# First weights in longer runs, fp32 filler matmuls, split and moved casts, and a reordered last product in a fused attention and FFN kernel

## The chip, the core and the metric

The kernel runs on one core of one Trainium2 chip. The time is that of the device in microseconds (us) for one execution of the whole kernel. A core has five engines that the text names: PE (TensorE, with its weight loads PEld), DVE (VectorE), ACT (ScalarE), POOL (GpSimd) and SP (SyncE), which here issues every DMA. PSUM is the memory that PE writes to; a "bank" below is one 2 KB slice of it in each of 128 partitions.

## The reference

Attention within chunks of 64 tokens, then a bilinear feed-forward layer on what it gives:

```python
# q, k, v: (8, 8, 576, 64) = batch, heads, sequence, head dim
scores = (1/8) * q_c @ k_c.T                     # per chunk of 64 tokens: 64 x 64
attn   = exp(scores - max) / (sum + 1e-9)
x      = (attn @ v_c) -> (4608 tokens, 512)      # heads side by side
out    = ((x @ w_a) * (x @ w_b)) @ w_out         # w_a, w_b: 512 x 1536, w_out: 1536 x 512
```

Inputs and outputs are fp32. The kernel multiplies in bf16 and accumulates in fp32.

## The kernel before, in words

**Tiling.** The 4608 tokens are nine blocks of 512. A block is two units of 256 tokens, and a unit is two groups of 128 tokens (two chunks of 64). Blocks 0 to 3 and 5 to 8 each take 512 tokens of one batch entry; block 4 collects the last 64 tokens of all eight, so that the loads of units 8 and 9 go in pieces of 64 partitions (`runs`), twice as many DMAs as elsewhere.

**Attention of a unit.** Q and k are loaded as fp32, cast to bf16 and turned, so that the head dimension lies on partitions. From unit 4 on a DMA transpose (`transpose_dma`, L215) turns them; units 2 and 3 are loaded two tokens to a partition (`load_pairs`) and turned on PE (`transpose_pairs`, L193, with copies out of PSUM in `evacuate_pairs`); block 0, units 0 and 1, is loaded four tokens to a partition and goes through its own `quad_` and `half_` functions. Scores go to PSUM tile PS (L233; L339 in block 0), ACT takes the exponential, PE sums it over keys with a matrix of ones (L250; `half_sums`, L351, in block 0), ACT takes the logarithm of the sums and the exponential of its negative, and DVE multiplies the values' product (PA; L266, L373) by this inverse (`normalise`, L285; `half_normalise`, L383). The result is xT, the transposed input of the next layer.

**Feed-forward.** `ffn` multiplies xT by one 128-wide tile of w_b and of w_a (four matmuls of 512 columns each, L397), ACT copies b out of PSUM (L408), and DVE multiplies a by it (L409). There are twelve such tiles in a block. Blocks 0 and 1 then multiply by w_out plainly (L419). From block 2 on `outs_fast` forms the output in seven half-size products in place of eight (L478), from sums of w_out that POOL made earlier (`sum_wo`) and sums of the products that DVE makes (`sum_ab`). In it ACT copies the products m3 and m4 to SBUF, POOL adds them to w (L496), DVE adds p1 to w, and further sums on DVE and POOL give the four quarters of the output. All products take their banks in turn from the ring F of four, so a bank must have been read before the fourth product after it.

**Order.** The program is written out by hand; every engine executes its instructions in the order written, and waits on semaphores. `slot(uv, us)` puts sums and values of unit uv and scores of unit us between two feature tiles. `cast_unit` casts q, k and v of a unit on POOL, `turn_unit` and `load_unit` issue DMAs on SP. In blocks 2 to 8 a slot at position i is followed by the casts of the next unit at i+1 and by its turn and the load of a further unit at i+3 (L836 to L843). SP issues in one order, so a DMA that waits holds up all later ones.

**Start.** SP issues q and k of block 0 (eight DMAs), v (eight), and the weights of pairs 0 and 1 (a pair is two feature tiles) in eight DMAs of 256 KB with runs of 128 columns, 512 bytes; pair 2 follows in two of 512 KB with runs of 256 columns, 1 KB. Weights go into a ring of ten staging slots, `wst`, and POOL casts them tile by tile (`land_half`, L171). PE meanwhile runs filler matmuls on zeros (`fill`, L522): eight at the start, one after the first transposes, four before the second values, two before the first feed-forward product. In units 2 and 3 casts are spread over POOL and DVE: DVE casts k of unit 2 in one piece (L732).

## Time and profile before

| | us |
|---|---|
| five runs | 316.63, 319.50, 319.71, 320.34, 320.47; median 319.71 |
| the profiled execution | 320.47 (one of the five) |
| its span, first to last instruction | 318.6 |
| outside the span | 1.87 |
| PE busy | 304.2 (95%) |
| DVE / ACT / POOL busy | 183.8 / 133.0 / 125.2 |
| DMA, mean over the span | 173 GB/s |
| mean granted clock of PE | 0.992 |

A group or timeline line reads: start, duration, engine, line of the program, operation, output and input, count, and in brackets how long the engine stood idle before it and what released it. A wait line gives the engine and line that waited, what it waited for, the total in us, how often, and the longest. A stretch line gives, for a window of time, busy us and count of each engine in the order PE, PEld, DVE, ACT, POOL, then the granted clock, the busy share of the DMA engines and GB/s. Busy times of matmuls that overlap in the pipeline are merged.

In the second view of the page, 40 slices of the span, the DMA engines show 90% or more in every slice from 8 to 151 us, and less after that. PE shows 70 to 79% in the first two slices and in the fifteenth (111.5 to 119.5 us), 40% in the last, and 90% or more in all others.

### The profile page before, as it was taken

How to read it: one execution, taken by the hardware profiler on the slowest of the kernel's cores; microseconds unless marked ns; L12 is line 12 of the kernel's file. 1: busy time of each engine (PE TensorE's matmuls, PEld its weight loads, DVE VectorE, ACT ScalarE, POOL GpSimd, SP SyncE). 2: the span in 40 equal slices, each digit the busy share in tenths (PEclk: the TensorE clock that was granted, in tenths of full speed). 3: DMA queues.
4: the chain of work that ended last, by engine and by line, in shares of the span. 5: the costliest groups of instructions: out<-in, count | busy, mean ns of one | idle time of the engine just before them, and what ended most of it. 6: DMA issues, size and time to landing. Idle time of an engine off the chain costs nothing.

```text
span 318.6 us, 7278 instructions
## 1 busy us (share of the span) xinstructions
PE 304.2 (95%) x2881; PEld 176.4 (55%) x2915; DVE 183.8 (58%) x368; ACT 133.0 (42%) x224; POOL 125.2 (39%) x161
## 2 busy tenths in 40 slices
PE   7799999999999979999999999999999999999994
PEld 3434446864444466446744674467446744674474
DVE  3433434534457743866587658764876476656662
ACT  3722217645236521645164516451645164413320
POOL 3657868977472145500660056005600400040022
PEclk9999999999999998999999999999999999999999
DMA  7999999999999999999299639962600210020003
GB/s 234 266 316 379 404 281 249 232 278 229 225 190 235 211 205 249 254 241 221 99 228 189 151 75 177 257 157 91 174 2 2 88 47 0 2 98 37 0 0 135
DMA packets 146899, 55.01 MB, mean 173 GB/s; under 512 B 126256, under 2 KB 140848, under 8 KB 146864
## 3 DMA queue, kind: packets, MB, share of 16 engines
q1 hardware_dynamic: 146864, 54.54, 68.9%
q8 instruction: 23, 0.38, 0.5%
q14 instruction: 12, 0.10, 0.1%
HBM read 37.75 MB, written 9.44 MB: 148 GB/s over the span
## 4 chain that ended last, share of the span: by engine, by line
PE 66%; SPq 17%; DMA 12%; issue 2%; POOL 2%; DVE 0%; POOLq 0%; DVEq 0%
PE F L397 43%; PE F L478 19%; SPq L123 10%; DMA wst<-in_moe_w_a_dram 5%; DMA f<-in_v_dram 3%; DMA f<-in_q_dram 3%; SPq L153 2%; SPq L131 2%; DMA qkT<-qkb 2%; SPq L146 2%; PE F L250 1%; SPq L139 1%; PE PS L233 1%; PE PA L266 1%; PE F L419 1%
## 5 line engine op out<-in xcount | busy, mean ns | idle before, releaser
L397 PE MATMUL F<-xT,wa 128*128 128x512 bf16 (+1 forms) x458 | 112.2, 366 | 0.8 <-POOL wa L171 0.3
L397 PE MATMUL F<-xT,wb 128*128 128x512 bf16 (+1 forms) x433 | 110.2, 366 | 1.7 <-POOL wb L171 0.6
L408 ACT CAST bsb<-F 128x512 bf16<-128x512 f32 (+1 forms) x115 | 64.0, 557 | 107.6 <-PE F L397 107.4
L409 DVE TENSOR_TENSOR ab<-F,bsb 128x512 bf16<-128x512 f32 (+1 forms) x115 | 75.4, 656 | 55.0 <-PE F L397 48.3
L397 PEld LDWEIGHTS <-wa 128*128 128x128 bf16 x460 | 44.7, 98 | 49.6 <-POOL wa L171 2.1
L397 PEld LDWEIGHTS <-wb 128*128 128x128 bf16 x460 | 43.3, 98 | 45.5 <-POOL wb L171 1.9
L496 POOL TENSOR_TENSOR part<-part 128x256 f32<-128x256 f32 x14 | 10.1, 724 | 130.3 <-ACT part L504 130.3
L171 POOL CAST qkb<-f 128x1024 bf16<-128x1024 f32 (+1 forms) x37 | 35.9, 980 | 26.5 <-DMA f<-in_k_dram 16.5
L478 PEld LDWEIGHTS <-wst 128*128 128x128 bf16 x420 | 41.5, 99 | 7.4 <-issue 2.2
L478 PE MATMUL F<-wst 128*128 128x256 bf16 x252 | 34.5, 276 | 2.0 <-DVE part L496 2.0
L285 DVE TENSOR_TENSOR xT<-PA,inv 128x512 bf16<-128x512 f32 x32 | 21.8, 684 | 16.6 <-ACT inv L280 16.6
L496 DVE TENSOR_TENSOR osb<-F,part 128x256 f32<-128x256 f32 x56 | 22.3, 420 | 10.7 <-POOL part L496 10.2
L171 POOL CAST vb<-f 128x1024 bf16<-128x1024 f32 (+2 forms) x22 | 19.9, 910 | 13.4 <-DMA f<-in_v_dram 9.5
L496 POOL TENSOR_TENSOR part<-part,osb 128x256 f32<-128x256 f32 x28 | 19.7, 725 | 12.2 <-DVE osb L496 12.2
L478 PE MATMUL F<-wst,ab 128*128 128x256 bf16 x168 | 24.0, 281 | 0.0
L276 ACT ACTIVATE lns<-F 128x512 f32<-128x512 f32 x32 | 17.4, 595 | 10.9 <-PE F L250 10.9
L419 PE MATMUL F<-wo,ab 128*128 128x512 bf16 x92 | 21.3, 379 | 0.4 <-issue 0.3
L496 DVE TENSOR_TENSOR part<-F,part 128x256 f32<-128x256 f32 x14 | 5.9, 425 | 26.4 <-POOL part L496 26.4
L467 DVE TENSOR_TENSOR wst<-ab 128x512 bf16<-128x512 bf16 x42 | 20.9, 497 | 0.0
L244 ACT ACTIVATE E<-PS 128x1024 bf16<-128x1024 f32 (+1 forms) x20 | 18.8, 942 | 4.9 <-PE PS L233 2.8
L478 PE MATMUL F<-wo,wst 128*128 128x256 bf16 x168 | 20.7, 273 | 0.0
L466 DVE TENSOR_TENSOR wst<-ab 128x512 bf16<-128x512 bf16 x42 | 20.1, 477 | 0.0
(48 smaller groups left out, 194.3 us busy)
## 6 DMA issues: line engine op xcount, KB each, us to landing
out_dram<-osb SPq DMA_DIRECT2D x31, 256.0 KB, 2.0
f<-in_q_dram SPq DMA_DIRECT2D x28, 256.0 KB, 4.0
f<-in_k_dram SPq DMA_DIRECT2D x28, 256.0 KB, 4.2
f<-in_v_dram SPq DMA_DIRECT2D x28, 256.0 KB, 4.4
wst<-in_moe_w_out_dram SPq DMA_DIRECT2D x6, 512.0 KB, 8.5
f<-in_v_dram SPq DMA_DIRECT2D x16, 128.0 KB, 3.6
wst<-in_moe_w_b_dram SPq DMA_DIRECT2D x4, 512.0 KB, 6.7
wst<-in_moe_w_a_dram SPq DMA_DIRECT2D x4, 512.0 KB, 7.9
```

The costliest lines, as they stand in the source:

```text
L123: eng.dma_start(out=t[p:p + n, g * 512:(g + 1) * 512].rearrange("p (h d) -> p h d", h=H), in_=src[b, :, s0:s0 + n, :].transpose([1, 0, 2]),)
L171: eng.tensor_copy(out=out, in_=in_)
L244: nc.scalar.activation(out=e[:, :, s], in_=PS[:, :, s], func=AF.Exp, scale=scale)
L285: nc.vector.tensor_tensor(out=x.rearrange("p m (g c t) -> p c g m t", g=2, c=2)[:, cl], in0=PA[:, cl, :].rearrange(shape, g=2, m=4), in1=i ...
L397: nc.tensor.matmul(bank[:, 0:n], w[ft // 2][ft % 2][:, kt, :], x[:, kt, us[0] * 256:us[0] * 256 + n], start=(kt == 0), stop=(kt == NKT - 1),)
L408: nc.scalar.copy(out=bT[:, 0:n], in_=banks[0][:, 0:n])
L409: nc.vector.tensor_tensor(out=ab[ft][:, us[0] * 256:us[0] * 256 + n], in0=banks[1][:, 0:n], in1=bT[:, 0:n], op=MULT)
L419: nc.tensor.matmul(o, ab[ft][:, tg * 128:(tg + 1) * 128], wo[ft // 2][:, ft % 2, :], start=(ft == 0), stop=(ft == NFT - 1),)
L466: nc.vector.tensor_tensor(out=y[:, 0:2], in0=a[:, 0:2], in1=a[:, 2:4], op=ADD)
L467: nc.vector.tensor_tensor(out=y[:, 2:4], in0=a[:, 1:3], in1=a[:, 0:4:3], op=SUB)
L478: nc.tensor.matmul(o, a(i)[:, c:c + 128], b(i), start=(i == 0), stop=(i == NP - 1))
L496: eng.tensor_tensor(out=out, in0=in0, in1=in1, op=op)
```

## The change

- The weights of pairs 0 and 1 are loaded in runs of 256 columns, as pair 2's were. Those of pair 0 are split by partitions in two DMAs each, b in 120 + 8, a in 104 + 24. The ring of staging slots starts at slot 4.
- `zero` is fp32 instead of bf16, so the fillers are fp32 matmuls. Eight become four, the one after the first transposes gets 128 columns, one is added before the first values, four become two, two become one.
- `half_sums` sums a whole half unit in four matmuls of 512 columns instead of eight of 256.
- The cast of k of unit 2 is split in two halves, on DVE and on ACT.
- The cast of v of unit 9, one instruction of POOL, is issued four steps later: after both fast output products of block 2, ahead of the casts of unit 10.
- In the last `outs_fast` (block 8, t = 1) the products come in another order: m3, m4, the two that need only these, then p1 and the last two. p1 is added on DVE to y1 and y2 instead of to w. Every other `outs_fast` keeps its order.

```diff
@@ -64,7 +64,7 @@
 
     identity = buf("identity", [128, 128], BF16)
     ones = buf("ones", [128, 64], BF16)
-    zero = buf("zero", [128, 512], BF16)
+    zero = buf("zero", [128, 512], FP32)
 
     NF32 = 3
     f32 = [[buf(f"f32_{i}_{x}", [128, 1024], FP32) for x in range(3)] for i in range(NF32)]
@@ -97,7 +98,7 @@
     asum = asum.rearrange("p (i n t) -> p i n t", i=NP, n=5)
     part = buf("part", [128, 2, 5, HF], FP32)
 
-    state = {"f": 0, "b": 0, "o": 0, "w": 0}
+    state = {"f": 0, "b": 0, "o": 0, "w": 4}
 
     def ring(name, bufs):
         i = state[name]
@@ -148,12 +149,14 @@
                 in_=v[0, 4 * hu:4 * hu + 4, g * 128:(g + 1) * 128, :].transpose([1, 0, 2]),
             )
 
-    def load_w(src, c0, n, eng):
+    def load_w(src, c0, n, eng, cut=128):
         st = ring("w", wst)
-        eng.dma_start(
-            out=st[:, 0:NKT * n].rearrange("p (kt c) -> p kt c", kt=NKT),
-            in_=src[:, c0:c0 + n].rearrange("(kt r) c -> r kt c", r=128),
-        )
+        for r in (slice(0, cut), slice(cut, 128)):
+            if r.start < 128:
+                eng.dma_start(
+                    out=st[r, 0:NKT * n].rearrange("p (kt c) -> p kt c", kt=NKT),
+                    in_=src[:, c0:c0 + n].rearrange("(kt r) c -> r kt c", r=128)[r],
+                )
         return st
 
     def load_wo(i, eng):
@@ -174,12 +177,15 @@
     def cast_qk(u, x, eng):
         copy(eng, qkb[u % 2][:, x, :], f32[u % NF32][x])
 
-    def cast_pairs(u, x, eng):
-        copy(
-            eng,
-            qkb[u % 2][:, x, :].rearrange("p (r h d) -> p h r d", r=2, h=H),
-            f32[u % NF32][x].rearrange("p (h r d) -> p h r d", h=H, r=2),
-        )
+    def cast_pairs(u, x, *engs):
+        n = 2 // len(engs)
+        for i, eng in enumerate(engs):
+            r = slice(n * i, n * i + n)
+            copy(
+                eng,
+                qkb[u % 2][:, x, :].rearrange("p (r h d) -> p h r d", r=2, h=H)[:, :, r],
+                f32[u % NF32][x].rearrange("p (h r d) -> p h r d", h=H, r=2)[:, :, r],
+            )
 
     def cast_v(u, eng, pieces=1):
         n = 1024 // pieces
@@ -344,14 +350,13 @@
                         stop=True,
                     )
 
-    def half_sums(hu, mm, SU):
-        s = slice(mm * 256, mm * 256 + 256)
+    def half_sums(hu, SU):
         for j in range(2):
             for cl in range(2):
                 nc.tensor.matmul(
-                    SU[j * 64:j * 64 + 64, cl, s],
+                    SU[j * 64:j * 64 + 64, cl, :],
                     ones[cl * 64:cl * 64 + 64, :],
-                    E[hu][cl * 64:cl * 64 + 64, j, s],
+                    E[hu][cl * 64:cl * 64 + 64, j, :],
                     start=True,
                     stop=True,
                 )
@@ -495,6 +500,24 @@
         def add(eng, out, in0, in1, op=ADD):
             eng.tensor_tensor(out=out, in0=in0, in1=in1, op=op)
 
+        if K == NBLK - 1 and t == 1:
+
+            A.copy(out=m3, in_=product(of_ab(0, 0), of_wsum(2)))
+            A.copy(out=m4, in_=product(of_ab(1, 1), of_wsum(3)))
+            add(G, w, m3, m4)
+            add(V, oa[:, HF:DM], product(of_asum(0), of_wo(1, 1)), m3)
+            add(G, y1, w, oa[:, HF:DM], SUB)
+            add(V, ob[:, 0:HF], product(of_asum(1), of_wo(0, 0)), m4)
+            add(G, y2, w, ob[:, 0:HF], SUB)
+            p1 = product(of_asum(4), of_wsum(4))
+            store(K, 2 + t, ob, 0, HF)
+            add(V, y1, p1, y1)
+            add(V, y2, p1, y2)
+            add(V, oa[:, 0:HF], product(of_asum(3), of_wsum(1)), y1)
+            store(K, t, oa)
+            add(V, ob[:, HF:DM], product(of_asum(2), of_wsum(0)), y2)
+            store(K, 2 + t, ob, HF)
+            return
         A.copy(out=m3, in_=product(of_ab(0, 0), of_wsum(2)))
 
         p4 = product(of_ab(1, 1), of_wsum(3), None, range(NP - 1))
@@ -508,19 +531,21 @@
         add(G, y1, w, oa[:, HF:DM], SUB)
         add(V, ob[:, 0:HF], product(of_asum(1), of_wo(0, 0)), m4)
         add(G, y2, w, ob[:, 0:HF], SUB)
-        halves = K == NBLK - 1 and t == 1
-        if halves:
-            store(K, 2 + t, ob, 0, HF)
         add(V, oa[:, 0:HF], product(of_asum(3), of_wsum(1)), y1)
         store(K, t, oa)
         add(V, ob[:, HF:DM], product(of_asum(2), of_wsum(0)), y2)
-        store(K, 2 + t, ob, HF if halves else 0)
-
-    def fill(n, bank=None):
-
-        for _ in range(n):
+        store(K, 2 + t, ob)
+
+    def fill(times, bank=None, n=512):
+
+
+        for _ in range(times):
             nc.tensor.matmul(
-                PA[:, 0, :] if bank is None else bank, zero[:, 0:128], zero, start=True, stop=True
+                PA[:, 0, 0:n] if bank is None else bank[:, 0:n],
+                zero[:, 0:128],
+                zero[:, 0:n],
+                start=True,
+                stop=True,
             )
 
     staged = {}
@@ -544,23 +569,18 @@
         for hu in range(2):
             load_half_v(hu, nc.sync)
 
-        def queue_half(i, h, ns):
-            for n in ns:
-                src = moe_w_a if n == "a" else moe_w_b
-                staged[n, i, h] = load_w(src, i * 256 + h * 128, 128, nc.sync), 0, 128
-
-        def queue_w(i):
-            for n, src in (("b", moe_w_b), ("a", moe_w_a)):
-                st = load_w(src, i * 256, 256, nc.sync)
+        def queue_w(i, cuts=(128, 128)):
+            for n, src, cut in (("b", moe_w_b, cuts[0]), ("a", moe_w_a, cuts[1])):
+                st = load_w(src, i * 256, 256, nc.sync, cut)
                 for h in range(2):
-                    staged[n, i, h] = st, h * 128, 256
+                    staged[n, i, h] = st, h * 128
 
         def land_half(n, i, h, eng):
-            st, c, w = staged[n, i, h]
+            st, c = staged[n, i, h]
             copy(
                 eng,
                 (wa if n == "a" else wb)[i][h],
-                st[:, 0:NKT * w].rearrange("p (kt c) -> p kt c", kt=NKT)[:, :, c:c + 128],
+                st.rearrange("p (kt c) -> p kt c", kt=NKT)[:, :, c:c + 128],
             )
 
         def land_w(i):
@@ -574,18 +594,18 @@
         def land_wo(i):
             copy(G, wo[i], staged["o", i].rearrange("p (f c) -> p f c", f=2))
 
-        for i in range(2):
-            for h in range(2):
-                queue_half(i, h, "ba")
+
+        queue_w(0, (120, 104))
+        queue_w(1)
         queue_w(2)
 
 
-        fill(8)
+        fill(4)
         quad_cast(0, 0, V)
         quad_turn(0, 0, A)
         quad_cast(0, 1, V)
         quad_turn(0, 1, V)
-        fill(1)
+        fill(1, n=128)
         for m in range(1, 4):
             for x in range(2):
                 quad_cast(m, x, G)
@@ -606,27 +626,26 @@
         quad_scores(2)
         expo(1, 0)
         quad_turn(3, 1, V)
-        half_sums(0, 0, PA)
-        half_sums(0, 1, PA)
+        half_sums(0, PA)
         half_log(PA)
         quad_scores(3)
         expo(1, 1)
         inverse(0)
+        spare = F[2]
+        fill(1, spare)
         half_values(0)
         for mm in range(2):
             half_normalise(0, mm)
-        half_sums(1, 0, PS)
-        half_sums(1, 1, PS)
+        half_sums(1, PS)
         half_log(PS)
         half_inverse(1, 0)
         half_inverse(1, 1)
         B0 = nextF(), nextF()
-        spare = F[2]
-        fill(4, spare)
+        fill(2, spare)
         half_values(1)
         for mm in range(2):
             half_normalise(1, mm)
-        fill(2, spare)
+        fill(1, spare)
         for of in "ba":
             ffn_products(0, 0, (0, 1), (0, 1), B0, of)
         for kt in range(2, NKT):
@@ -729,7 +748,7 @@
         cast_pairs(3, 1, G)
         some_sums(2)
         cast_unit(3, (2,))
-        cast_pairs(2, 1, V)
+        cast_pairs(2, 1, V, A)
         load_unit(5, (0,))
         o = nextF(), nextF()
         for ft in range(NFT):
@@ -837,7 +856,10 @@
                 if i in slots and slots[i] - 1 < NU:
                     slot(slots[i] - 1, slots[i] if slots[i] < NU else None)
                 if i - 1 in slots:
-                    cast_unit(slots[i - 1] + 1)
+
+                    cast_unit(slots[i - 1] + 1, (0, 1) if slots[i - 1] == 8 else (0, 1, 2))
+                if i - 5 in slots:
+                    cast_unit(slots[i - 5] + 1)
                 if i - 3 in slots:
                     turn_unit(slots[i - 3] + 1)
                     load_unit(slots[i - 3] + 3)
```

## The prediction, made before the changed kernel ran

> **What bounds the kernel now.** I read the page's busy shares first, then PE's waits, then the timeline round each wait, then the clock by stretch.
>
> ```profile
> PE 304.2 (95%) x2881; PEld 176.4 (55%) x2915; DVE 183.8 (58%) x368; ACT 133.0 (42%) x224; POOL 125.2 (39%) x161
> ```
>
> PE is the bound: time can only come from PE's idle time, from PE work that runs slowly, or from what lies after PE's last instruction. Of the waits from 40 to 120 us, three are for another engine or a DMA:
>
> ```profile
> PE F L478 <- DVE part L496: 2.0, 1, 2.0
> PE F L193 <- DVE osb L429: 0.7, 1, 0.7
> PE PS L233 <- DMA qkT<-qkb: 0.5, 2, 0.3
> ```
>
> The long one lies in the first fast output product of block 2. The timeline of POOL and PE there:
>
> ```profile
> 111.49 1.04 POOL L171 CAST qkb<-f 128x1024 bf16<-128x1024 f32 x1 [6.59 <-DMA f<-in_k_dram]
> 116.01 1.04 POOL L171 CAST vb<-f 128x1024 bf16<-128x1024 f32 x1 [3.48 <-DMA f<-in_v_dram]
> 117.01 0.72 POOL L496 TENSOR_TENSOR part<-part 128x256 f32<-128x256 f32 x1
> ...
> 118.24 0.81 PE L478 MATMUL F<-wst 128*128 128x256 bf16 x6 [2.00 <-DVE part L496]
> 118.89 2.25 PE L478 MATMUL F<-wst,ab 128*128 128x256 bf16 x11
> ```
>
> POOL's sum w = m3+m4 stands in POOL's order behind the cast of unit 9's v, and that cast waits 3.48 us for its DMA. Until w is there VectorE keeps a PSUM bank, and PE stands. The last line is the second half of the price: 11 matmuls in 2.25 us (205 ns each), where the same 11 take 1.36 us elsewhere. The clock by stretch says why:
>
> ```profile
> 118.00:120.00 2.00, 1.76 (x13) 1.44 (x13) 1.27 (x4) 0.00 (x0) 1.40 (x2) 0.80 1.11 252
> 120.00:122.00 2.00, 2.00 (x11) 1.34 (x10) 0.42 (x1) 0.37 (x1) 0.01 (x1) 0.50 1.07 331
> 122.00:124.00 2.00, 2.00 (x17) 1.67 (x16) 0.34 (x1) 0.37 (x1) 0.72 (x1) 0.85 1.07 172
> ```
>
> The column before the last two is the granted clock: it is halved for about 3.4 us after the stall. This pair of output products runs from 112.14 to 125.14, 13.0 us, where the chain that ended last shows 9.17 us for each later pair. So the place costs 3.83 us: 2.0 waited, 1.8 slow.
>
> The front is a second matter:
>
> ```profile
> 1.19 3.60 PE L522 MATMUL PA<-zero 128*128 128x512 bf16 x8 [1.19 <-DVE zero L536]
> 4.57 1.06 PE L316 MATMUL F<-identity,qkb 128*128 128x128 bf16 x8
> 5.43 0.64 PE L522 MATMUL PA<-zero 128*128 128x512 bf16 x1
> 6.42 0.46 PE L339 MATMUL PS<-qkT 64*64 64x64 bf16 x16 [0.36 <-DVE qkT L171]
> ```
>
> Eight fillers start 427 ns apart and hold PE until 4.57; q of the first quad has been cast by 3.88. From there the attention of unit pair 0 is a chain of short steps (6.42 to 16.86, VectorE's second normalisation), and weights arrive beside it: block 0's first six feature tiles wait several times for a cast that waits for a DMA, the last ending at 25.45. From there PE is dense until 44.9.
>
> **The change part by part.**
>
> *v of unit 9 cast later.* POOL's order becomes q, k of unit 9, the six sums of both output products, then v. The k cast ends at 112.53; w needs both ACT copies, at 114.57. So w runs at 114.6 to 115.3, VectorE's sum at 115.4 to 115.8, and the bank is wanted at 112.14 + 6 x 0.655 = 116.07. The wait goes, and with it the slow stretch: -3.83. Next to be late is the k cast (2.1 us of slack) and then the transposing DMA of unit 9. Behind the moved cast stand on POOL q and k of unit 10, wanted some 15 us later; v of unit 9 itself is first read at the second slot of block 3, about 13 us after. The transposing DMA stands on SP behind the first output's two stores, and those behind unit 10's v loads (issued until 118.60), which PE doesn't hold: it can issue at about 119.7 instead of 120.95 and, with the median 5.6 us to landing, lands at 125.3 (124.2 with the shortest, 4.5). PE now wants it at 129.38-3.83 = 125.55. Cost 0 taken, 0 to 1.5 us possible.
>
> *Fillers.* `zero` becomes fp32, twice the bytes: its memset goes from 0.27 to about 0.54 us, PE starts at 1.46. No fp32 matmul is in the trace. The nearest row is the bf16 filler, 427 ns cold: if an fp32 filler took that, four end at 3.2 and the front gains up to 1.3 us. [...] The 256-column sums joined to 512 stream the same columns (8 in 0.41): 0, between -0.1 and +0.1. [...]
>
> *First weights.* Pairs 0 and 1 (2.1 MB) come in 1 KB runs instead of 512 B. Before, the stretch 14 to 22 us moved 234 to 315 GB/s, the 1 KB stretch 22 to 26 us 351 to 360: 2.1 MB at 280 takes 7.5, at 350 6.0. The records of landing also show each transfer's sixteenth part 0.6 to 1.4 us behind the fifteenth. [...] The last weights of pair 2, at 24.72, land at about 12.4 + 3.15 MB / 340 GB/s + 0.6 = 22.3; the first `a` at about 16.2, cast by 16.8. [...] Front: +0.8, from -1.2 to +2.2. What is gained on DMA pulls later loads forward, and the ring starting at slot 4 takes SP's waits for casts away (2.4 and 0.9 us); PE doesn't see either.
>
> *k of unit 2.* VectorE's cast took 1.35 us (44.15) and stood ahead of two bank copies (1.27), for which the second transpose waited 0.67. Half of it takes about 0.43 to 0.68 (its 128x512 cast takes 0.43); ACT, idle for 8.47 us there, does the other in about 0.58. -0.6; with the front late the wait would have gone by itself, so it is -0.6 either way, once.
>
> *Lag absorbed.* PE then is 0.2 late at 63.85 and 108.3, where it waited 0.29 and 0.18 for transposing DMAs: -0.2, so PE reaches 112.1 unchanged.
>
> *Last output product.* Before, VectorE's chain POOL w, VectorE w, POOL y1, y2, VectorE ends at 315.81, with the last matmul done at about 314.5. Now p1 comes fifth, POOL's sums run during it, and after the last product only one VectorE add is left: three adds (0.4 each) from about 314.0 end at 315.2, and the stores, 0.33 each plus gaps on SP, follow. -0.45, from -0.7 to +0.1.
>
> Sum: -3.83 + 0.8 - 0.6 - 0.2 - 0.45 = **-4.3 us**. The profiled execution took 320.47 us (span 318.6) and is the slowest of the five; the difference carried to their median, 319.71, gives **315.4**. Changes under 1% (3.2 us) can hardly be told from none here: the five runs reach from 316.63 to 320.47.
>
> **The rivals.**
> *The fillers are shorter* (two passes, or the clock rises at once), and weights gate the front: -1.2 for +0.8, transposing DMAs absorb little since DMA is earlier too: about 313.5. For it: the front was DMA-bound. [...] 0.15.
> *A new wait takes the stall's place*: the transposing DMA of unit 9 lands 1 us after PE wants it, and a second half-clock stretch follows: +2, 317.5. For it: parity within 0.3 us by my count. 0.17.
> *The stall stays*, because k of unit 9 (ready 2.1 us early) slips behind PE: 319. 0.04.
> *Slower*: the filler itself. [...] 0.07.
>
> **How the numbers follow.** My case has 0.57, 314.0 to 316.8 by its own bounds. The range, 313.3 to 318.0, takes in the first two rivals. Under 316.5: most of my case and the first rival, 0.64; above 322.9: the slower rival, 0.07; between: 0.29.
>
> **What would show it.** Right: no PE wait for `part` in block 2, the POOL cast of `vb` after both products' sums, clock 1.00 from the front to the end, every pair of fast products 9.17; fp32 fillers about 1.7 us apart cold and 0.85 at full clock, transposes from about 7; weights of pair 2 landed by 22.5 and no PE wait for `wa`; no wait of L193 for `osb`. Wrong: transposes at or before 4.6 (first rival), a wait for `qkT` near 125.5 (second), the half clock beyond 9 us (slower).

## The result and the profile after

The changed kernel takes 317.82 us (median of 38 runs, 316.16 to 320.33), the kernel before 319.08 (75 runs, 316.02 to 322.73). The comparison gives a ratio of 0.9983, 95% interval 0.9967 to 1.0: about 0.5 us gained, no difference that counts. The medians lie further apart, 1.26 us, because the ratio compares means and leaves out runs more than 1.5% above the fastest of their kernel, nine of the kernel before and none of the changed one; the means of all runs are 319.09 and 318.22, 0.9 us apart. The prediction was 315.4, which is 4.3 us under the first median of before, 319.71.

In the two profiled executions the gain is larger: 320.47 us before, 317.68 after, spans 318.6 and 315.9. That gap between the profiles and the medians is half of this case. First the busy shares of the kernel after, from its page:

```profile
PE 305.2 (97%) x2877; PEld 177.6 (56%) x2910; DVE 184.3 (58%) x369; ACT 133.7 (42%) x225; POOL 124.8 (40%) x161
```

PE's waits, in the kernel after, whole span (who waits, for what, total us, times, longest):

```profile
PE PS L345 <- DVE qkT L174: 1.5, 3, 0.6
PE PA L543 <- DVE zero L561: 1.4, 1, 1.4
PE F L402 <- POOL wa L174: 1.3, 1, 1.3
PE PS L345 <- ACT qkT L172: 0.7, 1, 0.7
PE F L424 <- issue: 0.3, 2, 0.2
```

The waits for `part`, for `osb` and for the transposing DMAs (`qkT` by DMA) are no longer in the list; from the first plain output product on, only the two short waits for issue are left in it. What has grown is the third line, the first cast of `wa`: 1.3 us, where the list of before had 0.3 for all casts of `wa`. Lines of the program have moved by five or so: L402 is the feature tile, L483 the fast output product, L424 the plain one, L501 its sums, L174 the casts on POOL.

POOL and PE at the fast products of block 2, timeline of the kernel after:

```profile
111.04 1.04 POOL L174 CAST qkb<-f 128x1024 bf16<-128x1024 f32 x1 [7.31 <-DMA f<-in_k_dram]
116.09 0.72 POOL L501 TENSOR_TENSOR part<-part 128x256 f32<-128x256 f32 x1 [4.01 <-ACT part L527]
117.69 1.41 POOL L501 TENSOR_TENSOR part<-part,osb 128x256 f32<-128x256 f32 x2 [0.87 <-DVE osb L501]
120.68 0.73 POOL L501 TENSOR_TENSOR part<-part 128x256 f32<-128x256 f32 x1 [1.58 <-ACT part L527]
122.27 1.41 POOL L501 TENSOR_TENSOR part<-part,osb 128x256 f32<-128x256 f32 x2 [0.87 <-DVE osb L501]
123.63 1.04 POOL L174 CAST vb<-f 128x1024 bf16<-128x1024 f32 x1
```

POOL's sum w now waits only for ACT's copy, and the cast of unit 9's v comes after all sums. The clock there, in windows of 2 us (the granted clock is the third column from the end):

```profile
118.00:120.00 2.00, 2.00 (x21) 1.79 (x19) 0.85 (x2) 0.37 (x1) 1.10 (x2) 1.00 1.02 235
120.00:122.00 2.00, 2.00 (x21) 1.78 (x20) 0.56 (x2) 0.37 (x1) 0.73 (x1) 1.00 1.01 313
122.00:124.00 2.00, 1.95 (x14) 1.27 (x13) 1.23 (x4) 0.18 (x1) 1.73 (x3) 1.00 1.08 238
```

The pair runs from 113.59 to 122.76, 9.17 us for 13.0. The front of PE, from the timeline of the kernel after:

```profile
1.45 6.47 PE L543 MATMUL PA<-zero 128*128 128x512 f32 x8 [1.45 <-DVE zero L561]
7.75 0.61 PE L322 MATMUL F<-identity,qkb 128*128 128x128 bf16 x8
...
16.06 1.98 PE L543 MATMUL F<-zero 128*128 128x512 f32 x4
...
19.53 0.38 PE L402 MATMUL F<-xT,wb 128*128 128x512 bf16 x1
21.19 0.60 PE L402 MATMUL F<-xT,wa 128*128 128x512 bf16 x2 [1.27 <-POOL wa L174]
...
22.49 1.03 PE L402 MATMUL F<-xT,wb 128*128 128x512 bf16 x4
```

and POOL beside it:

```profile
16.93 0.61 POOL L174 CAST wb<-wst 128x512 bf16<-128x512 f32 x1 [2.06 <-DMA wst<-in_moe_w_b_dram]
20.52 0.61 POOL L174 CAST wa<-wst 128x512 bf16<-128x512 f32 x1 [2.98 <-DMA wst<-in_moe_w_a_dram]
```

An fp32 filler leaves two records, so eight records are four fillers. They hold PE until 7.75. The attention then ends at 19.85 (VectorE's second normalisation, 16.86 before), but the first `a` is cast only from 20.52, where it was 15.82. PE stands for it, and the second feature tile starts at 22.49 for 18.30.

The difference of the two profiled executions by stretch, from the starts of the same work in both:

| stretch | before | after | difference | predicted |
|---|---|---|---|---|
| start to first plain output product | 38.41 | 41.48 | +3.07 | +0.8 |
| to block 1 (k of unit 2) | 15.35 | 14.53 | -0.82 | -0.6 |
| to the fast products of block 2 | 58.38 | 57.58 | -0.80 | -0.2 |
| these two products | 13.00 | 9.17 | -3.83 | -3.83 |
| block 3 to the end | 193.46 | 193.14 | -0.32 | -0.45 |
| span | 318.6 | 315.9 | -2.7 | -4.3 |

### The profile page after: what moved, and what is told of

It reads as the page before. It is cut to its first block, busy times and chain, and to the rows that moved or that the text cites. A ratio compares the mean times of both kernels' runs of the same rounds, so it can differ in the third digit from the quotient of the medians.

```text
span 315.9 us, 7269 instructions
## 1 busy us (share of the span) xinstructions
PE 305.2 (97%) x2877; PEld 177.6 (56%) x2910; DVE 184.3 (58%) x369; ACT 133.7 (42%) x225; POOL 124.8 (40%) x161
## 4 chain that ended last, share of the span: by engine, by line
PE 89%; SPq 4%; DMA 2%; issue 1%; ACT 1%; POOL 1%; POOLq 0%; DVEq 0%; DVE 0%
PE F L402 59%; PE F L483 19%; PE F L424 6%; DMA wst<-in_moe_w_a_dram 2%; SPq L147 2%; PE F L256 2%; PE PS L239 2%; PE PA L272 1%; SPq L140 1%; POOL part L501 0%; SPq L156 0%; ACT lns L282 0%; ACT inv L286 0%; ACT qkT L172 0%; PE F L199 0%
## 5 line engine op out<-in xcount | busy, mean ns | idle before, releaser
L402 PE MATMUL F<-xT,wa 128*128 128x512 bf16 (+1 forms) x460 | 112.4, 366 | 1.6 <-POOL wa L174 1.3
L402 PE MATMUL F<-xT,wb 128*128 128x512 bf16 (+1 forms) x431 | 109.9, 366 | 1.2
L402 PEld LDWEIGHTS <-wa 128*128 128x128 bf16 x460 | 44.9, 98 | 50.0 <-POOL wa L174 1.8
L402 PEld LDWEIGHTS <-wb 128*128 128x128 bf16 x460 | 43.5, 98 | 44.7 <-issue 0.6
L501 POOL TENSOR_TENSOR part<-part 128x256 f32<-128x256 f32 x14 | 10.1, 724 | 131.0 <-ACT part L527 130.0
L174 POOL CAST qkb<-f 128x1024 bf16<-128x1024 f32 (+1 forms) x37 | 36.0, 983 | 28.7 <-DMA f<-in_k_dram 15.7
L483 PEld LDWEIGHTS <-wst 128*128 128x128 bf16 x420 | 41.1, 98 | 4.8
L483 PE MATMUL F<-wst 128*128 128x256 bf16 x252 | 33.3, 273 | 0.0
L501 DVE TENSOR_TENSOR osb<-F,part 128x256 f32<-128x256 f32 x56 | 22.3, 420 | 10.9 <-POOL part L501 9.4
L501 POOL TENSOR_TENSOR part<-part,osb 128x256 f32<-128x256 f32 x28 | 19.7, 725 | 11.4 <-DVE osb L501 11.3
L174 POOL CAST vb<-f 128x1024 bf16<-128x1024 f32 (+2 forms) x22 | 19.9, 910 | 7.4 <-DMA f<-in_v_dram 7.4
L483 PE MATMUL F<-wst,ab 128*128 128x256 bf16 x168 | 22.8, 273 | 0.0
L424 PE MATMUL F<-wo,ab 128*128 128x512 bf16 x92 | 21.3, 379 | 0.4 <-issue 0.3
L250 ACT ACTIVATE E<-PS 128x1024 bf16<-128x1024 f32 (+1 forms) x20 | 18.8, 942 | 4.8 <-PE PS L239 2.5
L483 PE MATMUL F<-wo,wst 128*128 128x256 bf16 x168 | 20.6, 273 | 0.0
L501 DVE TENSOR_TENSOR part<-F,part 128x256 f32<-128x256 f32 x15 | 6.4, 425 | 21.4 <-POOL part L501 21.4
```

What stands on the lines that cost most here:

```text
L174: eng.tensor_copy(out=out, in_=in_)
L250: nc.scalar.activation(out=e[:, :, s], in_=PS[:, :, s], func=AF.Exp, scale=scale)
L402: nc.tensor.matmul(bank[:, 0:n], w[ft // 2][ft % 2][:, kt, :], x[:, kt, us[0] * 256:us[0] * 256 + n], start=(kt == 0), stop=(kt == NKT - 1),)
L424: nc.tensor.matmul(o, ab[ft][:, tg * 128:(tg + 1) * 128], wo[ft // 2][:, ft % 2, :], start=(ft == 0), stop=(ft == NFT - 1),)
L483: nc.tensor.matmul(o, a(i)[:, c:c + 128], b(i), start=(i == 0), stop=(i == NP - 1))
L501: eng.tensor_tensor(out=out, in0=in0, in1=in1, op=op)
```

## The experiments

The theory after the result had three parts. (A) Removing the stall is worth what the profile says. (B) The first `a` comes late because it comes in one large transfer and because the split by partitions slows it. (C) The fp32 fillers cost little. The rivals were that the fillers alone set the front, that the split is harmless, and that the stall's removal gives its time back at a later wait. A "front" below is the start of the first plain output product, 38.41 in the profiled execution of before and 41.48 after. Ratios are to the kernel before on the same chip; the chips differ by up to 1.7 us in its median, so ratios and not medians are compared across groups of runs; versions on one chip are compared by their own times. Each profile is of a single execution, and the front of one kernel alone moves by over a microsecond from one to the next (38.41 to 39.61 in four profiles of the kernel before), so a difference of a few tenths between two profiles is not a measured effect.

### No split

```diff
-        queue_w(0, (120, 104))
+        queue_w(0)
```

> The changed kernel with pair 0's weights in two whole transfers of 128 partitions (1 KB runs kept). Theory, the split itself slows the loading: packets of 1 KB take about 46 ns from 13 us on instead of 66 to 80, the first a lands at about 17 instead of 20.4, no PE wait for wa, the second feature tile starts at about 21.2 instead of 22.49: 1.2 us less than the changed kernel. Rival, 1 KB runs are slow at this place whatever the split: a still lands after 20, the second tile still starts at 22.4 and the time is that of the changed kernel.

Measured: ratio 0.9877 (0.9834 to 0.992), median 317.34 of 6. The first `a` is cast from 19.05, 1.5 us earlier than with the split but 2 us later than expected, PE still waits 0.77 for it, and the front is 40.02. What the DMA moved says why. The kernel after, in windows of 2 us (the last column is GB/s):

```profile
14.00:16.00 2.00, 1.93 (x54) 0.92 (x54) 0.01 (x1) 2.00 (x3) 0.40 (x1) 1.00 0.99 248
16.00:18.00 2.00, 2.00 (x12) 0.70 (x8) 1.29 (x2) 1.85 (x4) 0.61 (x1) 1.00 1.06 232
18.00:20.00 2.00, 1.86 (x36) 0.80 (x36) 1.29 (x2) 0.46 (x1) 0.00 (x0) 1.00 1.09 267
```

and the same windows without the split:

```profile
14.00:16.00 2.00, 2.00 (x40) 0.85 (x39) 0.81 (x2) 1.88 (x3) 0.90 (x3) 1.00 1.03 320
16.00:18.00 2.00, 2.00 (x37) 0.82 (x35) 0.89 (x2) 1.45 (x3) 0.32 (x1) 1.00 1.00 299
18.00:20.00 2.00, 1.16 (x5) 0.28 (x5) 0.87 (x2) 0.00 (x0) 1.24 (x3) 1.00 1.08 364
```

The DMA engines are as busy in both, and move 232 to 267 GB/s with the split against 299 to 364 without. In the records of single packets a 1 KB packet takes 66 to 80 ns where the split transfers run (medians of each us from 15 to 19), and 46 ns without. So the split makes each packet slower; it doesn't leave engines idle.

Slower packets are not the whole of it. The two weights of pair 0 are 1024 packets of 1 KB. When the first `a` was cast, 1555 packets of weights had ended in the version without the split; with it that number was reached at 19.68, 0.6 us later, but the cast came another 0.8 us later, after 1846. So the larger part of the delay is order: with the split, packets of weights wanted later are moved ahead of pair 0's (0.84 MB by the time of the cast, 0.54 without).

Not all of the earlier front arrived later: this execution waited for unit 8's transposing DMA.

```profile
110.55 0.45 PE L239 MATMUL PS<-qkT 64*64 64x64 bf16 x32 [1.73 <-DMA qkT<-qkb]
```

### The fillers of before in the changed kernel, with and without the split

```diff
-    zero = buf("zero", [128, 512], FP32)
+    zero = buf("zero", [128, 512], BF16)
...
-        fill(4)
+        fill(8)
...
-        fill(1, spare)
...
-        fill(2, spare)
+        fill(4, spare)
...
-        fill(1, spare)
+        fill(2, spare)
```

(The single filler after the first transposes also has its 512 columns again.)

> The changed kernel with the fillers of before (eight, one, four, two, in bf16). Theory, the fp32 fillers hold the attention back: transposes start at 4.6 instead of 7.75, the second normalisation ends at about 17 instead of 19.85, but the split weights still land at 20.4, so the second tile starts at about 22.3: only 0.2 us less than the changed kernel, PE waiting over 3 us for wa, with a half-clock stretch in some runs. Rival, the weights land earlier when PE is earlier: 1.5 to 2 us less.

> The changed kernel with both undone: bf16 fillers as before, and pair 0 in whole transfers of 128 partitions with 1 KB runs. Theory: first a at about 16.5 to 17, second tile starts at 18.3 to 18.8, PE dense from there, 3.7 to 4.2 us less than the changed kernel: about 314. Rival of slow 1 KB runs: second tile after 21, 315.5 or more.

Measured with the split: 1.0006 (0.9974 to 1.0038), median 319.25 of 22. Without: 0.9871 (0.9828 to 0.9914), median 316.72 of 6. The two ran on one chip, so the split costs about 2.5 us between them. About 314 was expected without it, by a second tile at 18.3 to 18.8; it starts at 20.66. PE in the version with the split:

```profile
17.46 0.60 PE L402 MATMUL F<-xT,wb 128*128 128x512 bf16 x2 [1.02 <-POOL wb L174]
...
20.40 1.03 PE L402 MATMUL F<-xT,wa 128*128 128x512 bf16 x2 [2.34 <-POOL wa L174]
```

The attention was ready earlier (transposes at 4.57), so PE only stood longer, for `wb` and for `wa`; the clock was then halved from 18.34 to 25.17 and the front came at 43.03. Without the split:

```profile
19.35 0.60 PE L402 MATMUL F<-xT,wa 128*128 128x512 bf16 x2 [0.48 <-POOL wa L174]
...
20.66 1.03 PE L402 MATMUL F<-xT,wb 128*128 128x512 bf16 x4
```

The front came at 39.65, against 40.02 with fp32 fillers, though PE ran at half clock from 8.31 to 18.55 here and at full clock there. So without the split the choice of filler is worth 0.4 us between these profiles, within what one kernel varies, and nothing in the ratios (0.9871 and 0.9877). With it, fp32 fillers don't let the attention end sooner, but in these two profiles PE's idle time before `wa` is shorter with them (1.27 for 2.34).

### The v cast alone

Added to the kernel before:

```diff
-                    cast_unit(slots[i - 1] + 1)
+                    cast_unit(slots[i - 1] + 1, (0, 1) if slots[i - 1] == 8 else (0, 1, 2))
+                if i - 5 in slots:
+                    cast_unit(slots[i - 5] + 1)
```

> The kernel before with only the cast of unit 9's v moved. Theory: the PE wait for part (2.0 us) goes, and in the runs where the half clock followed it another 1.8: between 2.0 and 3.8 us less than before by the share of such runs. Rival, a wait for the transposing DMA of unit 9 takes its place: under 1 us less.

Measured: 0.9938 (0.9907 to 0.9968), median 318.55: 2.0 us gained, 1.0 to 3.0. In its timeline of PE:

```profile
109.87 0.45 PE L233 MATMUL PS<-qkT 64*64 64x64 bf16 x32 [0.89 <-DMA qkT<-qkb]
...
118.30 1.36 PE L478 MATMUL F<-wst,ab 128*128 128x256 bf16 x11
...
122.88 1.03 PE L397 MATMUL F<-xT,wb 128*128 128x512 bf16 x3
```

The wait for `part` is gone, the eleven matmuls take 1.36 us again, the pair 9.17 (113.71 to 122.88), and no wait for unit 9's transposing DMA took its place; the one for unit 8's, ahead of the pair, is 0.89 here and was 0.18 in the first profile of before. Yet the gain is 2.0 and not 3.83. The mechanism holds; the size in an ordinary run is smaller. So the question became how typical the stall of the profiled execution is.

### The changed kernel again

No edit: this asks how one kernel differs from execution to execution.

> The changed kernel itself, on the chip of the three runs beside it. Expected by both theories: 0.2 to 1% under before, the second tile starting at about 22.4, first a landing after 20.

Measured: 0.9949 (0.9922 to 0.9976), median 318.45 of 22. The profiled execution took 320.45 us. PE and the clock in its front:

```profile
22.26 0.60 PE L402 MATMUL F<-xT,wa 128*128 128x512 bf16 x2 [2.83 <-POOL wa L174]
...
23.96 1.91 PE L402 MATMUL F<-xT,wb 128*128 128x512 bf16 x4
25.67 1.47 PE L402 MATMUL F<-xT,wa 128*128 128x512 bf16 x4
```

```profile
22.00:24.00 2.00, 1.74 (x7) 0.72 (x8) 0.00 (x0) 0.23 (x1) 2.00 (x5) 0.79 1.01 349
24.00:26.00 2.00, 2.00 (x6) 0.70 (x5) 0.69 (x1) 0.45 (x2) 2.00 (x4) 0.50 1.08 382
```

Here `a` was cast from 21.59, PE stood 2.83 us, and the clock was then halved from 23.15 to 26.56, over feature tiles of which four matmuls took 1.91 us there and 1.03 at full clock. The sixth tile starts at 32.16 for 29.40: 1.07 for the later cast, 1.69 for the clock. In 8 of the 22 runs the mean granted clock is 0.992 to 0.995, as in this one, and these took 320.7 us on average, the others 318.2. So the late `a` has a second price, paid in about a third of the runs. And it was not slower packets that made `a` 1.07 us later in this execution: 1555 packets of weights had ended by 19.27, earlier than in the first profile, but `a` was cast only after 2373.

### Equal halves

```diff
-        queue_w(0, (120, 104))
+        queue_w(0, (64, 64))
```

> The changed kernel with pair 0's two weights split in 64 + 64 partitions instead of 120 + 8 and 104 + 24. [...] Rival, splitting as such, or two more DMAs, slows: packets of 66 to 80 ns again, a after 20, second tile at 22.4.

Measured: 0.9967 (0.9943 to 0.9991), median 318.62, the same as the changed kernel on that chip (318.45). In the timeline:

```profile
19.41 0.62 POOL L174 CAST wa<-wst 128x512 bf16<-128x512 f32 x1 [2.63 <-DMA wst<-in_moe_w_a_dram]
20.08 0.61 PE L402 MATMUL F<-xT,wa 128*128 128x512 bf16 x2 [0.61 <-POOL wa L174]
21.39 0.81 PE L402 MATMUL F<-xT,wb 128*128 128x512 bf16 x3
```

If it was the unequal parts (120 and 8, 104 and 24) that slowed the loading, packets, `a` and the second tile should come here as without a split (46 ns, 19.05, 21.03). The profile bears out the rival in part. Packets took 67 ns (median from 14 to 16 us), and the rate was 241 and 269 GB/s in the windows from 14 to 18 us, as the rival had it, so unequal parts are not needed to slow them. But `a` was cast from 19.41, only 0.36 later than in the profile without a split, and the second tile starts at 21.39, 0.36 later too. So the slower packets go with the split as such; how much of the later `a` in the changed kernel belongs to the unequal parts, one execution doesn't show. What in the path slows the packets stays open.

### Halves first, then 1 KB runs

Pair 0 comes as in the kernel before, in four transfers of 512 B runs; pairs 1 and 2 in whole transfers of 1 KB runs; fillers as before the change. The lines for the fillers and the staging slots are left out here.

```diff
-        queue_w(0, (120, 104))
+        for h in range(2):
+            for n, src in (("b", moe_w_b), ("a", moe_w_a)):
+                staged[n, 0, h] = load_w(src, h * 128, 128, nc.sync), 0, 128
```

> The changed kernel with the fillers of before, pair 0 in four transfers of one tile each (512 byte runs, as before the change) and pairs 1 and 2 whole in 1 KB runs. Theory, the front is set by how early the first b and a land and then by the rate: first products at about 15.8, second tile at about 18.3, dense from there, the sixth tile starting at about 25.3 where it started at 26.3 before: about 314 to 315, below both kernels. Rival, a floor further on: the transposing DMA of unit 8 makes PE wait near 108 by whatever the front gained, and the time is that without a split, 316 to 317.

Measured: 0.9915 (0.9888 to 0.9942), median 317.54. In PE's timeline:

```profile
17.58 0.60 PE L402 MATMUL F<-xT,wa 128*128 128x512 bf16 x2 [0.60 <-POOL wa L174]
...
108.74 0.45 PE L239 MATMUL PS<-qkT 64*64 64x64 bf16 x32 [1.50 <-DMA qkT<-qkb]
```

`a` is cast from 16.91 and the front is at 38.80, as early as in the kernel before. Against it stand the versions without a split (39.65 with bf16 fillers, 40.02 with fp32), where `a` was cast from 18.68 and 19.05: with whole 1 KB loads 1 MB must land before the first `a` can be used, where 0.5 MB was enough. What that alone costs the front these profiles don't separate: of the 0.85 to the version with bf16 fillers, part is its half clock up to 18.55, with the attention ending at 18.67 instead of 17.43. And 1.5 us of the gain ends in a wait for unit 8's transposing DMA; the time is 317.54, not the 314 to 315 expected, and the ratio is no better than without a split.

### The fillers alone

The kernel before with the fp32 fillers (the new form of `fill` and the filler of 128 columns after the first transposes are left out here):

```diff
-    zero = buf("zero", [128, 512], BF16)
+    zero = buf("zero", [128, 512], FP32)
...
-        fill(8)
+        fill(4)
...
+        fill(1, spare)
...
-        fill(4, spare)
+        fill(2, spare)
...
-        fill(2, spare)
+        fill(1, spare)
```

> The kernel before with only the fp32 fillers. Theory: transposes at 7 to 7.8 instead of 4.6, second normalisation at about 19.5 instead of 16.9, second tile at about 21 instead of 18.3, but weights have landed by then and the waits at the third to fifth tile vanish: the sixth tile at about 27.9 instead of 26.3, 1.5 us more than before in runs of like clock, and a mean clock of 0.995 or more in nearly every run. Rival, the clock kept up pays for the delay: same time or up to 1 us less than before.

Measured: 0.9963 (0.9937 to 0.999), median 319.57: 1.2 us less than before, 0.3 to 2.0. It was the rival that came, the clock that pays for the delay.

```profile
1.45 5.19 PE L522 MATMUL PA<-zero 128*128 128x512 f32 x8 [1.45 <-DVE zero L540]
...
118.85 0.81 PE L478 MATMUL F<-wst 128*128 128x256 bf16 x6 [0.60 <-DVE part L496]
```

The transposes start at 6.48 and the sixth tile 1.16 us later than in the profile of before. The four fillers end at 6.6 here, at 7.9 in the kernel after: the clock rose at 4.48 and at 7.05. So the term depends on where the rise falls. PE reached the fast products of block 2 2.0 us later than in the first profile of before, v of unit 9 was cast only 0.6 later (116.62 for 116.01), and PE lost 0.60 at the stall: a late front and the stall are not independent. The mean granted clock is 0.992 or more in all 22 runs. In the kernel before it goes from 0.976 to 1.0, and with bf16 fillers in the changed kernel from 0.971 to 0.995. Where the kernel before ran beside the experiments, the mean clock was under 0.99 in 78 of 125 runs, and on each of the three chips these took 1.5 to 2.4 us longer on average than those of 0.997 and more.

### A transposing DMA ahead of the stores

The version of halves and 1 KB runs (its edits are left out here), with unit 8's transposing DMA issued ahead of the four stores of block 1 in SP's order:

```diff
+        turn_unit(8)
         for tg in range(4):
```

> The version with pair 0 in halves and the bf16 fillers, and besides the transposing DMA of unit 8 issued ahead of block 1's four output stores instead of behind them. Theory, that DMA is a floor near 108 us that eats what the front gains: its issue comes 2.5 to 3 us earlier, the PE wait for it (1.50 in the run without this) goes, and the time falls by up to 1.5 us against that version, to a ratio to before of about 0.987. Rival, the DMA is late because the k that it turns is late or because the DMA engines are full: the wait stays over 1 us and the time the same.

Measured: 0.9944 (0.9919 to 0.997), median 316.68 of 19, lowest 314.67, span 313.7.

```profile
111.11 1.36 PE L483 MATMUL F<-wst,ab 128*128 128x256 bf16 x11
...
120.28 1.03 PE L402 MATMUL F<-xT,wb 128*128 128x512 bf16 x3
```

The wait near 108 is gone and the fast products start at 111.11 for 112.58, with the same front (38.79). This is the shortest span of all the profiles, and the version is faster than the kernel before. That the move did it is not shown. The DMA was issued 1.9 us earlier (99.81 for 101.72), but the version without a split and with bf16 fillers, which issued it behind the stores at 102.95, waited at most 0.2 us for it. And the ratio, taken on another chip, misses the 0.987 expected and does not stand apart from that of the version it came from.

### Three more executions of the kernel before

No edit: how typical is the stall that the prediction was built on?

> The kernel before, unchanged, one more profile. Theory, the stall of the first fast product of block 2 differs from run to run (PE's lateness against v's landing), and the half clock after it comes only in some: a wait for part between 0.5 and 2.5 us, and 9.17 plus that wait for the two products where the clock stays full. Rival, the profiled execution was typical: 2.0 us and half clock again.

> As the look before this one: theory, wait for part between 0.5 and 2.5 us, half clock after it in a minority of looks; rival, 2.0 us and half clock each time.

> As the two looks before this one: theory, wait for part between 0.5 and 2.5 us, half clock after it in a minority of looks; rival, 2.0 us and half clock each time.

Measured: 320.11, 316.80 and 321.63 us. First execution, PE:

```profile
119.63 0.82 PE L478 MATMUL F<-wst 128*128 128x256 bf16 x6 [1.83 <-DVE part L496]
120.28 1.36 PE L478 MATMUL F<-wst,ab 128*128 128x256 bf16 x11
```

Second execution, POOL:

```profile
114.09 1.04 POOL L171 CAST vb<-f 128x1024 bf16<-128x1024 f32 x1 [1.52 <-DMA f<-in_v_dram]
115.09 0.73 POOL L496 TENSOR_TENSOR part<-part 128x256 f32<-128x256 f32 x1
```

Third execution, PE:

```profile
119.50 0.81 PE L478 MATMUL F<-wst 128*128 128x256 bf16 x6 [2.33 <-DVE part L496]
120.15 2.41 PE L478 MATMUL F<-wst,ab 128*128 128x256 bf16 x11
```

In the first the stall came without the half clock; in the second the v cast was done at 115.1 and there was no listed wait, less than the 0.5 us expected at the least; in the third both came. With the profiled execution, the pair took 13.00, 11.17, 9.34 and 13.33 us, so 3.83, 2.00, 0.17 and 4.16 above 9.17: 2.5 on average. The fronts were 38.41, 39.61, 39.24 and 39.08.

The mean of these four executions against the mean of the two profiled ones of the changed kernel:

| stretch | before | after | difference |
|---|---|---|---|
| front | 39.09 | 42.86 | +3.8 |
| to the fast products of block 2 | 73.70 | 72.12 | -1.6 |
| these two products | 11.71 | 9.17 | -2.5 |
| block 3 to the end (the profiled pair) | 193.46 | 193.14 | -0.3 |
| sum | | | -0.7 |

That agrees with the 0.5 us (0 to 1.1) of the first comparison and is a little below the 1.6 (0.8 to 2.5) of the second. Four and two executions are few, but their fronts don't overlap (38.41 to 39.61 and 41.48 to 44.24), and the two products take 9.17 us in all nine profiles with the moved cast of v.

## Why the prediction was wrong, step by step

Two terms of the sum failed, and together they took nearly all of the forecast 4.3 us: the front, put at +0.8, came at +3.07 in the profiled pair and +3.8 in the means, and the stall, put at -3.83, is worth -2.5 in the mean of four executions. The first is the larger.

**The stall's size: the second step that failed.** The stall at the fast products was what the profile showed, and its two halves went as foreseen. What failed is carrying the difference of one execution to the median of five. The profiled execution had the earliest front of the four and the second worst stall; 3.83 was its value, and 2.5 is the mean of four. The cast of v alone gained 2.0 (1.0 to 3.0). The warning stood in the prediction, which called this execution the slowest of the five, but the sum used all of it.

**v of unit 9 cast later: right in its mechanism.** -3.83 in the profiled pair, for -3.83. Neither the k cast nor the transposing DMA of unit 9 became late: issued at 119.7 by the prediction, at 120.05 by the trace, with PE now 1.45 us later at these products than before.

**Fillers: later than taken.** The front's +0.8 holds the author's estimates of what an fp32 filler takes, of when the clock rises, and of how far the attention would fall back by both; no run shows that term. In the profile after, an fp32 filler of 512 columns takes 1.71 us at half clock (its two records start 0.853 apart) and 0.86 at full (0.429), four times what one in bf16 takes (0.427 and 0.215). With a bf16 filler's time as one pass, 1.45 to 7.05 at half clock is 13.1 passes of 427 ns, and from there to 7.75 at full clock 3.3 of 214, for the 16 of four fillers. The clock rose at 7.05 here, at 5.08 in the version without the split, 6.08 in the later execution and 4.48 in the version with the fillers alone; in the first profile of before it rose at 6.55, after 3.41 us in which PE was 89% busy. The transposes start at 7.75, where the prediction has them from about 7. The second normalisation came at 19.85, 3.0 later than the 16.86 of before, and the two fillers ahead of the second values took 1.98.

**First weights: the step that failed most.** `a` was to land at 16.2 and be cast by 16.8; it was cast from 20.52, and from 21.59 in the later execution. The error has two parts. First, the landing time itself: 16.2 counted the rate of 1 KB runs but not that a whole transfer has to land before any of it is cast. Without the split the cast still starts at 18.7 to 19.1, with halves at 16.9, and the last weights of pair 2, put at 22.3, land at 24.1 and 24.4 without the split and at 25.4 in the profile after; in the kernel before it was 24.7. Second, the split was taken for a small gain, an estimate from the sixteenth part of a transfer, which in the profile of before landed 0.6 to 1.4 us behind the fifteenth in the last two transfers of v and the first two of weights, and 0.2 to 0.5 in most of the weights after them. No run shows a gain: beside the versions without it, the split of the change delays `a` by 1.0 to 1.5 us in the pairs with the same fillers and 2.5 in the later execution (0.4 with 64 + 64), by slower packets and by the order in which they come. That the attention would end after the weights, as the +0.8 has it, was therefore wrong: it ended at 19.85 and the weights were later still.

From one profile to the next the front goes 38.80 with halves and bf16 fillers, 39.65 with whole 1 KB loads, 40.02 with fp32 fillers, 41.48 with the split; only the last step is borne out by times on one chip (2.5 us between the two versions with bf16 fillers); the first two are within what one kernel varies. The later execution adds 1.07 for landing and 1.69 for a half-clock stretch. The forecast of +0.8, with +2.2 as its bound, reached neither.

**The half clock came back elsewhere.** The prediction asked for clock 1.00 from the front to the end. The wait for `wa` brought the slow stretch back in about a third of the runs, at the first feature tiles instead of the fast products.

**k of unit 2: right.** -0.82 in its stretch, of which the vanished wait is 0.67.

**Lag absorbed: too small.** Two waits for transposing DMAs (0.29 and 0.18) are gone as foreseen, and the stretch gains 0.8 in the profiled pair. The other executions of before show why it can be more: one waited 1.1 there. In an execution where PE waits for unit 7's or 8's, a later front loses less than its lag, and an earlier one gains less than its lead (1.73 and 1.50 in two versions with an earlier front than the changed kernel). The time of that wait is not fixed: unit 8's DMA was issued at 105.18 in the first of these, at 101.72 in the second, and at 102.95 in the version without a split and with bf16 fillers, where PE hardly waited.

**Last output product: right, a little large.** VectorE ends 0.60 us after the last matmul in place of 1.28, which is 0.68 gained, but from there to the end takes 3.15 instead of 2.79; -0.32 is left for -0.45. In the other profiles with the new order the stretch from block 3 to the end takes 192.97 to 193.40, with the old one 193.45 or 193.46, so the gain goes from 0.05 to 0.5.

**The rivals.** None of them came: the fillers did not shorten the front, nor hold the clock down (it rose at 7.05), and no wait for unit 9's transposing DMA took the stall's place. That the second rival's 317.5 lies near the 317.82 measured is luck, as its wait never came. The case that did come, weights that land after the attention, was not among them; it was ruled out by the landing time of 16.2.

## What to carry to other kernels

Before a stall is taken out of a profile at its full price, profile the same kernel several times: where a wait depends on a DMA's landing, and a half-clock stretch on that wait, one execution can show the extreme (3.83 us here, for 2.5 in the mean of four). A faster transfer rate isn't an earlier first tile; ask how many bytes must land before the first consumer can start, keep those transfers small and over all partitions (the first `a` was cast from 16.91 with halves and 18.68 whole, both with bf16 fillers, and from 19.05 whole and 20.52 split, both with fp32), and use long runs for what follows. A wait of 2 to 3 us of PE at a dense stretch may cost twice, once for itself and once for the clock after it (2.00 us here, then 3.41 at half clock, which cost another 1.8).

## What the runs showed of the hardware

- **Split transfers have slower packets, and later weights overtake them.** 120 + 8 and 104 + 24: 66 to 80 ns for 1 KB; 64 + 64: 67; all 128: 46. The engines were as busy in all three. When pair 0's 1024 packets had landed and the first `a` was cast, 1846 and 2373 packets of weights had ended with the split of the changed kernel, 1766 with 64 + 64, 1555 and 1636 without.
- **The half clock came in whole multiples of 3.41 us.** The stretches in the traces last 3.41 us (120.29 to 123.70 in the third execution of before; 23.15 to 26.56 in the later one of the changed kernel), twice that (18.34 to 25.17, bf16 fillers with the split) or three times (8.31 to 18.55, without it). The changes between them lie whole multiples apart as well: in the first profile of before the rise at 6.55 and the fall at 119.19 are 112.64 us apart, 33 times 3.413, and in the profile after the rise at 7.05 and the fall at 314.25 are 307.20 apart, 90 times.
- **Whether half clock followed a stall went with PE's busy share.** A window below is 3.41 us long and ends a multiple of 3.413 from the execution's clock changes. PE was busy for 41% of the window that held the stall of 2.00 us, 32% with 2.33, 26% with 2.83 and 43% of the window that ends as the one of 2.34 begins, and the clock was halved; it was busy for 46% with 1.83, 49% with 1.73 and 56% with 1.50, and the clock stayed. Each of the three long stalls for `part` (2.00, 2.33, 1.83) fell within one window, so it was their length and not their phase that told them apart. In the first 9 us, where PE runs transposes and 64-wide matmuls, windows 43% (first of the three executions of before), 49% (v cast alone) and 55% busy (bf16 fillers without the split) were followed by half clock too, so this share is not the whole measure.
- **fp32 fillers keep the clock up through a sparse front; what that is worth depends on what follows.** With bf16 fillers the attention ends at 16.86 to 17.43 in profiles at full clock and at 18.67 to 19.80 in the three where the clock was halved from about 8 to 18.5 us; with fp32 fillers it ends at 18.57 to 19.85, always at full clock, from a start 2 to 3 us later. In the kernel before the fillers alone gained 1.2 us; in the version without the split, with the cast of v moved, nothing.
